# Attention block: first rows of maxima by TensorE transposes, a lead of 16 products, two half query groups moved into the loop, weight pieces held behind gathers

## The chip, the cores and the metric

The kernel runs on one core of a Trainium2 chip. The time is the device time of one execution in microseconds. The engines are TensorE (PE, matrix products), VectorE (DVE), ScalarE (ACT), GpSimd (POOL) and SyncE (SP, which issues transfers here). The profile is of one execution.

## The reference

One transformer block with conditioning: sequence 2048, width 512, 32 heads of 16 with one shared key and value head, and an inner width of 1376.

```
mod = (silu(c) @ w_mod).reshape(...)          # sa, ca, ga, sb, cb, gb
h = layernorm(x) * (1 + ca) + sa
q = (h @ wq) as 32 heads of 16;  k = h @ wk;  v = h @ wv
o = softmax(q k^T / sqrt(16)) v;  x = x + ga * (o @ wo)
h = layernorm(x) * (1 + cb) + sb
x = x + gb * (gelu(h @ w1 + b1) @ w2 + b2)
```

All is fp32. The kernel multiplies with numbers split in a high and a low part (names that end in H and L).

## The kernel before

**The units.** The attention is cut into 64 units: 8 blocks of 256 query rows, times 8 groups of 4 heads. A unit is worked in eight K steps. In a step PE computes four maximum products m (L507, queries times keys, only to find each row's maximum), which DVE reduces one by one (L512), and four score products e (L612), which ACT turns into exponentials (L616); sixteen accumulate instructions (L633) multiply these with the values. An e needs the row maxima inside its query operand: `qst` holds a unit's queries, and its partition rows 48 and 49 hold the negative maxima's high and low parts, so that the product subtracts them. The maximum products therefore run ahead of the scores by a lead, and the lead is made before the loop starts.

**From the maxima to the rows.** When all products of a unit are reduced, `put_max` orders: a DVE reduce to `mm` (L560), a 32x32 transpose to `turned` (L561), a gather on POOL to `mt` and its split to `mh` and `ml` (L555, L130, L137), and four transfers that SP issues into `qst` (L550). `later(n, f)` puts f off by n ticks of a clock that runs two to a K step. `MAX_WAIT` gives the waits ahead of gather and send.

**What sets the order.** Every engine works through its instructions in the order in which the program records them. SP's transfers stand in one row as well: one that waits holds all behind it. Beside the steps run other jobs as batches of matmuls in pieces: query projections (`qproj_late`), the output projection, transposes tp of the normalised rows xh, and the MLP's products w1ps and w2ps. A block's second layernorm, ahead of the MLP, runs on DVE (statistics, L840, L846) and POOL (ve, rs, xh, L847 to L852); tp reads xh, one half of the block's rows after the other.

**Weights in pieces.** The MLP's and output weights are loaded, scaled and split on POOL piece by piece inside the loop, one turn every `PREP` = 4 ticks. A turn loads one piece (for the last, narrower piece a POOL MEMSET ahead of the load, L1133, L1134) and splits an earlier one (L1137, L130, L137). The pieces share three buffers.

**The prologue.** Ahead of the loop, `SLOTS` deals the key and query projections, the small conditioning products (modl) and the first maximum products onto PE. `FIRST_MAX` orders the products of units 0 and 1, in pairs. `WARM[3]` filler matmuls (idle) stand ahead of the loop. The program before makes 56 maximum products there, the lead of `LEAD` = 6 groups of four behind unit 0's 32.

Of the kernel before, what the change touches and what calls it, by code (L numbers as in the profile page):

```python
# [14 lines left out]
P = 128  # L15
# [5 lines left out]

LEAD = 6
LEAD_0 = 6
FIRST_MAX = ((0, 0), (1, 0), (0, 1), (1, 1), (0, 2), (0, 3), (1, 2), (1, 3))
SLOTS = ((2, "keys 1", "keys 1"), (2, "keys 1", "keys 1"), (2, "low 1", "heads 2"), (2, "heads 2", "k 1"), (1, "warm"), (1, "heads 2"), (2, "heads 2", "v 0"),
# [4 lines left out]
MAX_WAIT = (1, 4)  # L30
QBUFS = 4
# [7 lines left out]
NORM_WAIT = 6  # L39
WARM = (4, 16, 2, 5)  # L40
MOD_WAIT = 3
# [9 lines left out]
def adaln_mqa_mlp(  # L51
# [88 lines left out]
    clock = [0]  # L140
    state = {"mods": False, "q": NB * KD, "busy": False, "turns": 1}
    pending = []
# [216 lines left out]

    def xhat1(b, eng):  # L360

        mv, rs, nm = hts_stats[b]
        xt = xts[b]
        for t in range(QT):
            if eng is nc.scalar:
# [50 lines left out]

    def send_q(b, g, qH, qL):
        for t, src in enumerate((qH, qL)):
            nc.sync.dma_start(out=dq[b][g][t].rearrange("a r j n -> (a r j) n"), in_=raw(src))
        state["q"] -= 1  # L420
        sent.add((b, g))

    sent = set()

    def qpairs(b, g):
        hH, hL = hts[b]
        gs = slice(g * P, (g + 1) * P)
        return [(wqH[:, k, gs], wqL[:, k, gs], hH[:, k, :], hL[:, k, :]) for k in range(KD)]

    def qtiles(b, g):  # L430
        qH = att.tile([P, BQ], F32R, name=f"qH{b}_{g}", tag="xH", bufs=2)
        qL = att.tile([P, BQ], F32R, name=f"qL{b}_{g}", tag="xL", bufs=2)
        return qH, qL
# [34 lines left out]
    def load_q(u):  # L468
# [5 lines left out]
        cols = slice(r0 % BQ, r0 % BQ + w)  # L474
        assert (h, g) in sent
        for s in range(2):
# [5 lines left out]
    class Max:  # L482


        def __init__(self):
# [45 lines left out]
    def put_max(u, mx):  # L531
# [13 lines left out]
        def send():  # L545
            for s in range(2):
                for r, src in ((48, mh), (49, ml)):
                    dst = qst[64 * s + r:64 * s + r + 1].rearrange("p j (t n) -> p (j t) n", n=P)
                    ring = nc.scalar if u == 0 and s else nc.sync
                    ring.dma_start(out=raw(dst), in_=raw(src[2 * T * s:2 * T * (s + 1), :].unsqueeze(1)))  # L550
            placed.add(u)
# [7 lines left out]
        def reduce():  # L559
            nc.vector.tensor_reduce(out=mm[:, :4 * T], in_=mx, axis=AX.X, op=ALU.max)  # L560
            nc.vector.transpose(out=turned, in_=mm)  # L561
# [669 lines left out]
    def q_group():  # L1231
        for i in range(KD):
            next(projections[0])
            if i == KD - 1:
                next(projections.pop(0))
            yield

    def warm():
# [24 lines left out]
    mod1(0, 3, act, dve)  # L1263
    rows = xhat1(1, act)
    run(rows, 2)

    def first_q(t):
        if t == 1:
            run(q_group())
            load_q(0)  # L1270
            load_q(1)

    stats1(2, first_q)
    run(rows)
    run(keys(0))
    low_k(0)
# [5 lines left out]
    def last_h(t):  # L1282
        if t == QT - 1:
# [9 lines left out]
            "v 0": one(v_out, 0), "v 1": one(v_out, 1), "v 2": one(v_out, 2), "v 3": one(v_out, 3), "rows": late_rows(),  # L1293
            "low 1": one(low_k, 1), "low 2": one(low_k, 2), "low 3": one(low_k, 3), "k 1": one(repeat_k, 1), "k 2": one(repeat_k, 2), "k 3": one(repeat_k, 3), "load": one(load_q, 2), "warm": warm(),
            "wq 1": one(prep_wq, 1), "wq 2": one(prep_wq, 2), "wq 3": one(prep_wq, 3)}
# [49 lines left out]
    def end_step(u, K):  # L1345

        pv(u, K)
        if K == steps[u] - 1:
            finish_unit(u)
            if units[u][1] == NQ - 1:  # L1350
                put_off(rest(units[u][0], units[u][0] == len(blocks) - 1))

    keep_warm(WARM[3], tag="e2", bufs=1)
    behind = None
    bare = [False]
    for u in range(NU):
        for K in range(0, steps[u], 2):
# [163 lines left out]
```

## Time and profile before

| | us |
|---|---|
| runs | 1563.49, 1561.64, 1562.66 (median 1562.66) |
| the profiled execution's own time | 1561.89 |
| its span in the trace | 1560.1 |
| PE busy | 1543.2 |
| DVE busy | 1400.8 |
| ACT busy | 1227.4 |
| POOL busy | 681.5 |

The times below are microseconds from the span's start. A row of a timeline gives the start, the time it took, the engine, the line of the code, the operation, output<-input, the shape of both, and how many alike instructions it joins; in square brackets how long the engine had been idle before, and what ended that. SPq is SP's queue, and its time is that of the issue with its waiting. A row of windows gives the stretch, its length, busy time and count of each engine, the granted TensorE clock, the share of the transfer engines and GB/s. With a line chosen, it counts that line alone.

### The profile page before, as it was taken

How to read it: one execution, taken by the hardware profiler on the slowest of the kernel's cores; microseconds unless marked ns; L12 is line 12 of the kernel's file. 1: busy time of each engine (PE TensorE's matmuls, PEld its weight loads, DVE VectorE, ACT ScalarE, POOL GpSimd, SP SyncE). 2: the span in 40 equal slices, each digit the busy share in tenths (PEclk: the TensorE clock that was granted, in tenths of full speed). 3: DMA queues.
4: the chain of work that ended last, by engine and by line, in shares of the span. 5: the costliest groups of instructions: out<-in, count | busy, mean ns of one | idle time of the engine just before them, and what ended most of it. 6: DMA issues, size and time to landing. Idle time of an engine off the chain costs nothing.

```text
span 1560.1 us, 41350 instructions
## 1 busy us (share of the span) xinstructions
PE 1543.2 (99%) x16347; PEld 955.2 (61%) x16347; DVE 1400.8 (90%) x2479; ACT 1227.4 (79%) x2392; POOL 681.5 (44%) x1194
## 2 busy tenths in 40 slices
PE   7999999999999999999999999999999999999999
PEld 4456555567655665557655675556655676556657
DVE  7999999999999999999999999999999999999725
ACT  5577778788878887788877887788877888778953
POOL 5545433867322570246522562245611474225721
PEclk9999999999999999999999999999999999999999
DMA  7225412312030211202012120302112120211241
GB/s 250 92 93 197 148 56 85 124 52 97 19 109 19 83 59 36 94 28 99 30 54 76 55 86 23 109 14 100 44 49 80 46 97 17 84 55 63 84 159 52
DMA packets 83125, 121.61 MB, mean 78 GB/s; under 512 B 19614, under 2 KB 56222, under 8 KB 82676
## 3 DMA queue, kind: packets, MB, share of 16 engines
q1 hardware_dynamic: 82916, 118.97, 22.9%
q8 instruction: 129, 2.11, 0.6%
q14 instruction: 64, 0.52, 0.1%
q10 hardware_dynamic: 16, 0.00, 0.0%
HBM read 91.13 MB, written 27.27 MB: 76 GB/s over the span
## 4 chain that ended last, share of the span: by engine, by line
PE 84%; DVE 10%; issue 3%; POOL 2%; DMA 1%; ACT 1%; SPq 0%; POOLq 0%; DVEq 0%
PE acc L633 28%; PE m L507 24%; PE e L612 15%; DVE mx L512 8%; PE w1ps L193 8%; PE w2ps L183 2%; PE w1ps L183 1%; DMA xt<-in_A_x_dram 1%; PE w2ps L193 1%; PE qps L193 1%; PE tp L193 1%; PE wops L193 1%; PE kps L162 1%; DVE st L840 1%; DVE x L833 1%
## 5 line engine op out<-in xcount | busy, mean ns | idle before, releaser
L512 DVE TENSOR_REDUCE mx<-m 128x1 f32<-128x512 f32 x2048 | 1269.3, 681 | 87.7 <-PE m L507 64.7
L616 ACT ACTIVATE p<-e 128x512 f32<-128x512 f32 x2048 | 1098.0, 598 | 254.8 <-PE e L612 106.4
L507 PE MATMUL m<-ks,qst 64*128 64x512 f32 x2048 | 832.9, 429 | 2.0 <-DVE mx L512 0.6
L612 PE MATMUL e<-qst,ks 64*128 64x512 f32 x2048 | 739.9, 413 | 0.0
L633 PE MATMUL acc<-p,va 128*32 128x256 f32 x8192 | 548.0, 385 | 0.0
L507 PEld LDWEIGHTS m<-ks,qst 64*128 64x128 f32 x2048 | 367.1, 184 | 211.6 <-DVE mx L512 174.0
L612 PEld LDWEIGHTS e<-qst,ks 64*128 64x128 f32 x2048 | 358.7, 185 | 92.3 <-ACT p L616 64.0
L633 PEld LDWEIGHTS acc<-p,va 128*32 128x32 f32 x8192 | 214.5, 109 | 213.7 <-issue 110.7
L555 POOL TENSOR_SCALAR mt<-turned 8x32 f32<-8x32 f32 x256 | 53.1, 208 | 419.5 <-DVE turned L561 407.4
L193 PE MATMUL w1ps<-h2H,w1t 64*128 64x256 f32 x1216 | 232.7, 287 | 0.0
L193 PEld LDWEIGHTS w1ps<-h2H,w1t 64*128 64x128 f32 x1216 | 183.6, 185 | 28.4 <-issue 14.4
L193 PE MATMUL w1ps<-h2L,w1t 64*128 64x256 f32 x608 | 167.0, 275 | 0.0
L193 PE MATMUL w2ps<-w2H,gH 64*128 64x512 f32 x264 | 115.9, 439 | 0.0
L193 PEld LDWEIGHTS w1ps<-h2L,w1t 64*128 64x128 f32 x608 | 112.8, 185 | 0.0
L193 PE MATMUL w2ps<-w2L,gH 64*128 64x512 f32 x264 | 103.4, 392 | 0.0
L193 PE MATMUL w2ps<-w2H,gL 64*128 64x512 f32 x264 | 103.0, 390 | 0.0
L959 POOL TENSOR_SCALAR tt<-tt 128x256 f32<-128x256 f32 x77 | 31.0, 403 | 143.1 <-ACT tt L958 109.8
L137 POOL TENSOR_TENSOR gL<-z,gH 128x256 fp32r<-128x256 f32 x77 | 56.9, 739 | 6.4
L960 POOL TENSOR_TENSOR tt<-tt,z 128x256 f32<-128x256 f32 x77 | 56.8, 738 | 6.4
L970 POOL TENSOR_TENSOR z<-tt,z 128x256 f32<-128x256 f32 x77 | 56.4, 733 | 6.0
L969 POOL TENSOR_TENSOR tt<-tt,z 128x256 f32<-128x256 f32 x77 | 56.5, 734 | 0.0
L193 PE MATMUL wops<-woH,onH 64*128 64x512 f32 x112 | 49.8, 444 | 0.0
(190 smaller groups left out, 1495.3 us busy)
## 6 DMA issues: line engine op xcount, KB each, us to landing
w1t<-dw SPq DMA_DIRECT2D x82, 512.0 KB
qst<-dq SPq DMA_DIRECT2D x384, 32.0 KB
do<-oc SPq DMA_DIRECT2D x64, 128.0 KB
dw<-w1s SPq DMA_DIRECT2D x11, 512.0 KB
xt<-in_A_x_dram SPq DMA_DIRECT2D x4, 1024.0 KB
dq<-qH SPq DMA_DIRECT2D x16, 256.0 KB
dq<-qL SPq DMA_DIRECT2D x16, 256.0 KB
x<-in_A_x_dram SPq DMA_DIRECT2D x8, 512.0 KB
```

The costliest lines, as they stand in the source:

```text
L137: eng_l.tensor_tensor(out=dst_l, in0=src, in1=raw(dst_h), op=ALU.subtract)
L183: nc.tensor.matmul(ps, a, b_, start=first_, stop=last_)
L193: ins = nc.tensor.matmul(ps, a[rows], b_[rows], start=first_ and s == 0, stop=last_ and s == 1)
L507: nc.tensor.matmul(m, qsts[u][rows, j, t * P:(t + 1) * P], ks[rows, kc * 512:(kc + 1) * 512], start=True, stop=True)
L512: nc.vector.tensor_reduce(out=self.mx[u][:, i, kc:kc + 1], in_=m, axis=AX.X, op=ALU.max)
L555: nc.gpsimd.tensor_scalar(out=mt[:, g:g + 32], in0=turned[g:g + 4 * T, :], scalar1=1.0, scalar2=0.0, op0=ALU.mult, op1=ALU.add)
L612: nc.tensor.matmul(e, ks[rows, kt * P:(kt + 1) * P], rhs, start=True, stop=True)
L616: ins = nc.scalar.activation(dst, e, AF.Exp, scale=0.25)
L633: ins = nc.tensor.matmul(accs[u][32 * cidx:32 * cidx + 32, :], va[:, kt, :], rhs, start=kt == 0, stop=kt == NKT - 1)
L960: nc.gpsimd.tensor_tensor(out=tt, in0=tt, in1=z, op=ALU.mult)
L969: nc.gpsimd.tensor_tensor(out=tt, in0=tt, in1=z, op=ALU.mult)
L970: nc.gpsimd.tensor_tensor(out=z, in0=tt, in1=z, op=ALU.add)
```

## The change

- `LEAD` goes from 6 to 4 groups: 48 products are made before the loop, not 56.
- `FIRST_MAX` gets counts, so that a part of a group can wait, and `SLOTS` a new order.
- Unit 0's rows no longer go over POOL and transfers: DVE writes mm and its rounding remainder into a cleared tile `spots`, four PE transposes (`rows0`) bring them to rows 48 and 49, and one DVE add puts these into `qst`.
- Query groups 0 and 1 of the first 512 rows are projected only for 256 columns before the loop; the other halves become two jobs of the loop.
- The gather is ordered directly behind the transpose, and the send two ticks later.
- A weight turn that comes due while a unit's maxima wait for their reduce (`closing`) is put off by one tick, behind the reduce and the gather.
- The filler matmuls ahead of the loop go; the first query and key projections alternate; the last slice of the second 512 rows' first layernorm goes to POOL.

```diff
-LEAD = 6
-LEAD_0 = 6
-FIRST_MAX = ((0, 0), (1, 0), (0, 1), (1, 1), (0, 2), (0, 3), (1, 2), (1, 3))
+LEAD = 4
+LEAD_0 = 4
+FIRST_MAX = ((0, 0, 4), (1, 0, 4), (0, 1, 4), (1, 1, 3), (0, 2, 4), (0, 3, 4), (1, 1, 1), (1, 2, 4), (1, 3, 4))
 SLOTS = ((2, "keys 1", "keys 1"), (2, "keys 1", "keys 1"), (2, "low 1", "heads 2"), (2, "heads 2", "k 1"), (1, "warm"), (1, "heads 2"), (2, "heads 2", "v 0"),
          (2, "heads 3"), (2, "heads 3"), (2, "heads 3"), (2, "heads 3"), (0, "keys 2"), (2, "keys 2"), (2, "keys 2"), (2, "keys 2"),
          (2, "low 2", "k 2", "v 1", "wq 1"), (0, "keys 3"), (2, "keys 3"), (2, "keys 3"), (2, "keys 3"), (2, "low 3", "k 3"),
-         (0, "v 2"), (2, "q 1"), (2, "q 1"), (2, "q 1"),
-         (2, "q 1", "rows"), (2, "v 3", "wq 2"), (2, "rows"), (2, "rows"), (2, "rows", "wq 3", "load"))
-MAX_WAIT = (1, 4)
+         (0, "v 2", "q 1", "q 1", "spots"), (2, "q 1", "q 1"), (2, "q 1"), (2, "rows", "wq 2"), (2, "wq 3"),
+         (2, "rows", "load"), (2, "v 3", "rows", "first", "rows"))
+MAX_WAIT = 2
...
-WARM = (4, 16, 2, 5)
+WARM = (4, 16, 2, 0)
...
     def qproj(b, g):
 
-        ps = psum.tile([P, BQ], F32, name=f"qps{b}_{g}", tag="v" if g else "x")
-        yield from mm3(ps, qpairs(b, g), 3, 1)
-        qH, qL = qtiles(b, g)
+        part = slice(0, HQ)
+        ps = psum.tile([P, HQ], F32, name=f"qps{b}_{g}", tag="v" if g else "x")
+        yield from mm3(ps, qpairs(b, g, part), 3, 1)
+        qH, qL = qtiles(b, g, part)
         if g == 0:
             nc.scalar.copy(qH, ps)
             nc.vector.tensor_tensor(out=qL, in0=ps, in1=raw(qH), op=ALU.subtract)
         else:
-            q32 = pro.tile([P, BQ], F32, name=f"q32_{b}_{g}", tag="h32", bufs=4)
+            q32 = pro.tile([P, HQ], F32, name=f"q32_{b}_{g}", tag="h32", bufs=4)
             nc.scalar.copy(q32, ps)
-            split(qH, qL, q32, act, pool)
-        send_q(b, g, qH, qL)
+            nc.scalar.copy(qH, q32)
+            yield -2
+            nc.gpsimd.tensor_tensor(out=qL, in0=q32, in1=raw(qH), op=ALU.subtract)
+        send_q(b, g, qH, qL, part)
         yield -2
 
-    def qproj_late(b, g):
-        ps = psum.tile([P, BQ], F32, name=f"qps{b}_{g}", tag="x")
-        size_ = BATCH if (b, g) < LONG else SHORT
-        yield from batches(ps, qpairs(b, g), size_)
-        q32 = wts_pool["rest"].tile([P, BQ], F32, name=f"q32_{b}_{g}", tag="ot", bufs=2)
+    def qproj_late(b, g, part=slice(0, BQ)):
+        w = part.stop - part.start
+        ps = psum.tile([P, w], F32, name=f"qps{b}_{g}_{part.start}", tag="x")
+        size_ = BATCH * BQ // w if (b, g) < LONG else SHORT
+        yield from batches(ps, qpairs(b, g, part), size_)
+        q32 = wts_pool["rest"].tile([P, w], F32, name=f"q32_{b}_{g}_{part.start}", tag="ot", bufs=2)
         if size_ == SHORT:
             nc.scalar.copy(q32, ps)
         else:
             nc.vector.tensor_copy(out=q32, in_=ps)
-        qH, qL = qtiles(b, g)
+        qH, qL = qtiles(b, g, part)
         split(qH, qL, q32, nc.gpsimd, nc.gpsimd)
-        later(4, lambda: send_q(b, g, qH, qL))
+        later(4, lambda: send_q(b, g, qH, qL, part))
...
-            begin = [o for u, kc in FIRST_MAX for o in products(u, [kc])]
+            parts = {(u, kc): products(u, [kc]) for u in range(2) for kc in range(NKC)}
+            begin = [parts[u, kc].pop(0) for u, kc, n in FIRST_MAX for _ in range(n)]
+            assert not any(parts.values())
...
+        if u == 0:
+            nc.vector.tensor_reduce(out=mm[:, :4 * T], in_=mx, axis=AX.X, op=ALU.max)
+            src = mm[:, :4 * T].rearrange("p (s n) -> p s n", s=2)
+            dst = spots.rearrange("p n (s c) -> p s n c", s=2)
+            nc.vector.tensor_copy(out=dst[:, :, :, 48], in_=src)
+            nc.vector.tensor_tensor(out=dst[:, :, :, 49], in0=src, in1=raw(dst[:, :, :, 48]), op=ALU.subtract)
+            return
         turned = att.tile([P, 32], F32, name=f"turned{u}", tag="turned", bufs=2)
-        if u == 0:
+        if u == 1:
...
-                    ring = nc.scalar if u == 0 and s else nc.sync
-                    ring.dma_start(out=raw(dst), in_=raw(src[2 * T * s:2 * T * (s + 1), :].unsqueeze(1)))
+                    nc.sync.dma_start(out=raw(dst), in_=raw(src[2 * T * s:2 * T * (s + 1), :].unsqueeze(1)))
...
             nc.vector.transpose(out=turned, in_=mm)
-            later(MAX_WAIT[0], gather)
-            later(MAX_WAIT[1], send)
+            gather()
+            state["closing"] = False
+            later(MAX_WAIT, send)
 
 
         if NQ <= u < NQ + 2:
             reduce()
         else:
+            state["closing"] = True
             later((0 - clock[0]) % 4 + 1, reduce)
+
+    spots = pro.tile([P, 4, P], F32R, name="spots")
+
+    def clear():
+        nc.gpsimd.memset(raw(spots), 0.0)
+
+    def first_rows():
+
+        qst = qsts[0].rearrange("p j n -> p (j n)")
+        ps = psum.tile([P, BQ], F32, name="rows0", **ebank())
+        for n in range(4):
+            nc.tensor.transpose(ps[:, n * P:(n + 1) * P], raw(spots[:, n, :]), ident)
+        nc.vector.tensor_tensor(out=qst, in0=ps, in1=raw(qst), op=ALU.add)
+        placed.add(0)
...
-    late = late[len(late) - len(projections):]
+    assert len(projections) == len(late) - 2
+    late = late[2:4] + [qproj_late(0, g, slice(HQ, BQ)) for g in range(2)] + late[4:]
...
+    def prepare_turn():
+        for _ in range(state["turns"]):
+            if weights and next(preps[weights[0]], 0) == 0:
+                weights.pop(0)
...
-                for _ in range(state["turns"]):
-                    if weights and next(preps[weights[0]], 0) == 0:
-                        weights.pop(0)
+                if state["closing"]:
+                    later(1, prepare_turn)
+                else:
+                    prepare_turn()
```

First place: DVE at the end of the prologue. mx0 are unit 0's maxima, m0 and m1 the products of units 0 and 1. Before:

```order
L512 TENSOR_REDUCE mx0_483<-m0_1_1_3_0_815 128x1
L512 TENSOR_REDUCE mx0_483<-m0_1_1_3_1_818 128x1
L560 TENSOR_REDUCE mm0_193<-mx0_483 128x8
L561 STREAM_TRANSPOSE turned0_821<-mm0_193 128x32
L512 TENSOR_REDUCE mx1_545<-m1_0_0_2_0_843 128x1
L512 TENSOR_REDUCE mx1_545<-m1_0_0_2_1_846 128x1
```

After:

```order
L520 TENSOR_REDUCE mx0_484<-m0_1_1_3_0_809 128x1
L520 TENSOR_REDUCE mx0_484<-m0_1_1_3_1_812 128x1
L547 TENSOR_REDUCE mm0_193<-mx0_484 128x8
L550 CAST spots_197<-mm0_193 128x2x4
L551 TENSOR_TENSOR spots_197<-mm0_193,spots_197 128x2x4
L520 TENSOR_REDUCE mx1_546<-m1_1_1_1_0_828 128x1
L520 TENSOR_REDUCE mx1_546<-m1_1_1_1_1_831 128x1
L598 TENSOR_TENSOR qst0_158<-rows0_844,qst0_158 128x512
L520 TENSOR_REDUCE mx1_546<-m1_0_0_2_1_868 128x1
```

The transpose to turned0 is gone, three operations into mm0 and spots take its place, and the add of rows0 stands two reduces later.

Second place: POOL around block 0's second layernorm (ve0_0 to xh2_0_0). mt11 to ml11 are unit 11's gather, w2f8 and w2f6 weight pieces. Before:

```order
L555 TENSOR_SCALAR mt11_4472<-turned11_4471 8x32 x4
L130 TENSOR_SCALAR mh11_4473<-mt11_4472 8x128
L137 TENSOR_TENSOR ml11_4474<-mt11_4472,mh11_4473 8x128
L1137 TENSOR_TENSOR w2f8_4398<-w2f8_4398,gb_83 128x512
L130 TENSOR_SCALAR w2H_3816<-w2f8_4398 128x512
L137 TENSOR_TENSOR w2L_3817<-w2f8_4398,w2H_3816 128x512
L1133 MEMSET w2f10_4580 128x512
L847 TENSOR_SCALAR ve0_0_4222<-mv0_0_4220 128x2
L849 TENSOR_TENSOR rs0_0_4221<-ve0_0_4222,mhalf_64 128x2
L852 TENSOR_SCALAR xh2_0_0_4218<-x1_0_4210,mv0_0_4220,rs0_0_4221 128x512 x2
```

After:

```order
L569 TENSOR_SCALAR mt11_4577<-turned11_4576 8x32 x4
L130 TENSOR_SCALAR mh11_4578<-mt11_4577 8x128
L137 TENSOR_TENSOR ml11_4579<-mt11_4577,mh11_4578 8x128
L1167 TENSOR_TENSOR w2f6_4419<-w2f6_4419,gb_83 128x512
L130 TENSOR_SCALAR w2H_3986<-w2f6_4419 128x512
L137 TENSOR_TENSOR w2L_3987<-w2f6_4419,w2H_3986 128x512
L877 TENSOR_SCALAR ve0_0_4229<-mv0_0_4227 128x2
L879 TENSOR_TENSOR rs0_0_4228<-ve0_0_4229,mhalf_64 128x2
L882 TENSOR_SCALAR xh2_0_0_4225<-x1_0_4217,mv0_0_4227,rs0_0_4228 128x512 x2
```

The gather and one weight piece still stand in a row ahead of ve0_0, but two K steps of products lie between unit 11's maxima before and now; the piece is w2f6, since later ones were put off, and the MEMSET of w2f10 is gone from here.

Third place: that MEMSET, on POOL around unit 12's gather, and on SP the transfers that follow it. POOL after:

```order
L569 TENSOR_SCALAR mt12_4916<-turned12_4915 8x32 x4
L130 TENSOR_SCALAR mh12_4917<-mt12_4916 8x128
L137 TENSOR_TENSOR ml12_4918<-mt12_4916,mh12_4917 8x128
L1167 TENSOR_TENSOR w2f7_4505<-w2f7_4505,gb_83 128x512
L130 TENSOR_SCALAR w2H_3986<-w2f7_4505 128x512
L137 TENSOR_TENSOR w2L_3987<-w2f7_4505,w2H_3986 128x512
L1167 TENSOR_TENSOR w2f8_4626<-w2f8_4626,gb_83 128x512
L130 TENSOR_SCALAR w2H_3986<-w2f8_4626 128x512
L137 TENSOR_TENSOR w2L_3987<-w2f8_4626,w2H_3986 128x512
L1163 MEMSET w2f10_4977 128x512
```

SP before:

```order
L651 DMA do1_115<-oc0_1266 128x256
L550 DMA qst0_158<-mh12_4811 1x4x128
L550 DMA qst0_158<-ml12_4812 1x4x128
L550 DMA qst0_158<-mh12_4811 1x4x128
L550 DMA qst0_158<-ml12_4812 1x4x128
```

SP after:

```order
L681 DMA do1_115<-oc0_1231 128x256
L1164 DMA w2f9_4972<-in_B_w2_dram 128x512
L1164 DMA w2f10_4977<-in_B_w2_dram 96x512
L564 DMA qst0_158<-mh12_4917 1x4x128
L564 DMA qst0_158<-ml12_4918 1x4x128
```

In SP's row the loads of w2f9 and w2f10 moved from ahead of unit 11's sends (mh11) to ahead of unit 12's (mh12). The load of w2f10 writes the tile that the MEMSET clears, which POOL reaches behind unit 12's gather and the pieces w2f7 and w2f8.

More of the change, by code (lines that the diff above doesn't have):

```diff
@@ L140, in adaln_mqa_mlp @@
     clock = [0]
-    state = {"mods": False, "q": NB * KD, "busy": False, "turns": 1}
+    state = {"mods": False, "q": NB * KD + 2, "busy": False, "turns": 1, "closing": False}
     pending = []
@@ L358, in stats1, with xhat1 @@
         hts_stats[b] = mv, rs, nm
-    def xhat1(b, eng):
+    def xhat1(b, eng, last=None):
         mv, rs, nm = hts_stats[b]
@@ L364, in xhat1 @@
         for t in range(QT):
+            eng = last if last and t == QT - 1 else eng
             if eng is nc.scalar:
@@ L415, in v_out, with send_q, qpairs, qtiles @@
         nc.scalar.copy(va[:, b * QT:(b + 1) * QT, 0:Dh], pv_[:, :, 16:32])
-    def send_q(b, g, qH, qL):
+    def send_q(b, g, qH, qL, part):
         for t, src in enumerate((qH, qL)):
-            nc.sync.dma_start(out=dq[b][g][t].rearrange("a r j n -> (a r j) n"), in_=raw(src))
+            nc.sync.dma_start(out=dq[b][g][t][:, :, :, part].rearrange("a r j n -> (a r j) n"), in_=raw(src))
         state["q"] -= 1
-        sent.add((b, g))
+        sent.update((b, g, n) for n in range(part.start, part.stop, HQ))
     sent = set()
-    def qpairs(b, g):
+    def qpairs(b, g, part):
         hH, hL = hts[b]
         gs = slice(g * P, (g + 1) * P)
[L428 to L433, printed above, removed]
+        return [(wqH[:, k, gs], wqL[:, k, gs], hH[:, k, part], hL[:, k, part]) for k in range(KD)]
+    def qtiles(b, g, part):
+        w = part.stop - part.start
+        qH = att.tile([P, BQ], F32R, name=f"qH{b}_{g}_{part.start}", tag="xH", bufs=2)
+        qL = att.tile([P, BQ], F32R, name=f"qL{b}_{g}_{part.start}", tag="xL", bufs=2)
+        return qH[:, :w], qL[:, :w]
     def qproj(b, g):
-        ps = psum.tile([P, BQ], F32, name=f"qps{b}_{g}", tag="v" if g else "x")
-        yield from mm3(ps, qpairs(b, g), 3, 1)
-        qH, qL = qtiles(b, g)
+        part = slice(0, HQ)
+        ps = psum.tile([P, HQ], F32, name=f"qps{b}_{g}", tag="v" if g else "x")
+        yield from mm3(ps, qpairs(b, g, part), 3, 1)
+        qH, qL = qtiles(b, g, part)
         if g == 0:
@@ L443, in qproj @@
         else:
-            q32 = pro.tile([P, BQ], F32, name=f"q32_{b}_{g}", tag="h32", bufs=4)
+            q32 = pro.tile([P, HQ], F32, name=f"q32_{b}_{g}", tag="h32", bufs=4)
             nc.scalar.copy(q32, ps)
-            split(qH, qL, q32, act, pool)
-        send_q(b, g, qH, qL)
+            nc.scalar.copy(qH, q32)
+            yield -2
+            nc.gpsimd.tensor_tensor(out=qL, in0=q32, in1=raw(qH), op=ALU.subtract)
+        send_q(b, g, qH, qL, part)
         yield -2
-    def qproj_late(b, g):
-        ps = psum.tile([P, BQ], F32, name=f"qps{b}_{g}", tag="x")
-        size_ = BATCH if (b, g) < LONG else SHORT
-        yield from batches(ps, qpairs(b, g), size_)
-        q32 = wts_pool["rest"].tile([P, BQ], F32, name=f"q32_{b}_{g}", tag="ot", bufs=2)
+    def qproj_late(b, g, part=slice(0, BQ)):
+        w = part.stop - part.start
+        ps = psum.tile([P, w], F32, name=f"qps{b}_{g}_{part.start}", tag="x")
+        size_ = BATCH * BQ // w if (b, g) < LONG else SHORT
+        yield from batches(ps, qpairs(b, g, part), size_)
+        q32 = wts_pool["rest"].tile([P, w], F32, name=f"q32_{b}_{g}_{part.start}", tag="ot", bufs=2)
         if size_ == SHORT:
@@ L474, in load_q @@
         cols = slice(r0 % BQ, r0 % BQ + w)
-        assert (h, g) in sent
+        assert (h, g, cols.start) in sent
         for s in range(2):
@@ L1234, in q_group @@
             if i == KD - 1:
-                next(projections.pop(0))
+                last = projections.pop(0)
+                next(last)
             yield
+        next(last, None)
+        yield
     def warm():
@@ L1263, in adaln_mqa_mlp @@
     mod1(0, 3, act, dve)
-    rows = xhat1(1, act)
-    run(rows, 2)
+    first_group, first_keys = q_group(), keys(0)
+    for _ in range(KD - 1):
+        next(first_group)
+        next(first_keys)
     def first_q(t):
         if t == 1:
-            run(q_group())
+            run(first_group)
             load_q(0)
             load_q(1)
+            run(xhat1(1, act, pool))
+            run(first_keys)
     stats1(2, first_q)
-    run(rows)
-    run(keys(0))
     low_k(0)
@@ L1293, in adaln_mqa_mlp @@
             "v 0": one(v_out, 0), "v 1": one(v_out, 1), "v 2": one(v_out, 2), "v 3": one(v_out, 3), "rows": late_rows(),
-            "low 1": one(low_k, 1), "low 2": one(low_k, 2), "low 3": one(low_k, 3), "k 1": one(repeat_k, 1), "k 2": one(repeat_k, 2), "k 3": one(repeat_k, 3), "load": one(load_q, 2), "warm": warm(),
+            "low 1": one(low_k, 1), "low 2": one(low_k, 2), "low 3": one(low_k, 3), "k 1": one(repeat_k, 1), "k 2": one(repeat_k, 2), "k 3": one(repeat_k, 3), "load": one(load_q, 2), "warm": warm(), "first": one(first_rows), "spots": one(clear),
             "wq 1": one(prep_wq, 1), "wq 2": one(prep_wq, 2), "wq 3": one(prep_wq, 3)}
```

## The prediction

> **What bounds the kernel now.** I read the page's busy times and chain first.
>
> ```profile
> span 1560.1 us, 41350 instructions
> PE 1543.2 (99%) x16347; PEld 955.2 (61%) x16347; DVE 1400.8 (90%) x2479; ACT 1227.4 (79%) x2392; POOL 681.5 (44%) x1194
> PE 84%; DVE 10%; issue 3%; POOL 2%; DMA 1%; ACT 1%; SPq 0%; POOLq 0%; DVEq 0%
> ```
>
> PE is busy 99% of the span, so the loop ends when PE's instructions have been issued one after another; POOL is idle more than half the time but can still be late at one place. The next view, windows that count the accumulate instructions (16 to a K step), gives a step's price.
>
> ```profile
> 253.44:284.79 31.35, 12.84 (x192) 5.02 (x193) 1.00 0.35 111
> 339.89:396.90 57.01, 21.42 (x321) 8.38 (x321) 1.00 0.26 90
> 1471.10:1476.29 5.19, 2.14 (x33) 0.84 (x33) 1.00 0.02 4
> ```
>
> 192 accumulates are 12 plain steps: 31.35 / 12 = 2.61 us. 320 are 20 steps with twelve 256-column matmuls beside them: 57.01 / 20 = 2.85. Two late steps that have no maximum products left but the same twelve cost 5.19. The third figure from the right is the granted clock, 1.00.
>
> The third view is the engines' timelines where the prologue ends, with the tensor-engine row that I use for a transpose.
>
> ```profile
> 27.54 0.66 PE L375 MATMUL tp<-ident,xt 128*128 128x128 f32 x4 [1.25 <-ACT h L381]
> ...
> 60.62 5.22 DVE L512 TENSOR_REDUCE mx<-m 128x1 f32<-128x512 f32 x8
> 66.89 2.48 DVE L512 TENSOR_REDUCE mx<-m 128x1 f32<-128x512 f32 x4 [1.05 <-PE m L507]
> 69.40 0.19 DVE L560 TENSOR_REDUCE mm<-mx 128x8 f32<-128x32 f32 x1
> 69.93 1.01 POOL L555 TENSOR_SCALAR mt<-turned 8x32 f32<-8x32 f32 x4 [0.32 <-DVE turned L561]
> 72.14 0.61 SPq L550 DMA_DIRECT2D qst<-ml  x1
> 73.59 1.43 PE L287 MATMUL idle<-wkH 128*128 128x512 f32 x5
> 74.95 0.49 PE L612 MATMUL e<-qst,ks 64*128 64x512 f32 x2
> ```
>
> Reduces run at 5.22 / 8 = 0.65 us nearly back to back: before the loop VectorE paces, not PE. Unit 0's rows take from 69.40 to the end of the sends (72.75 here), and the first score e stands at 74.95, behind five filler matmuls.
>
> **The prologue.** All of unit 0's maxima are reduced at the 46th product instead of the 48th, and the split query groups and the later place of the small matmuls take the 1.05 us hole out of VectorE's row: the reduce mm moves from 69.40 to about 69.40 − 2 × 0.65 − 1.05 = 67.0. Then three small DVE operations (0.2 each, by the mm row), four PE transposes (0.66, the row at 27.54) behind the two products and one group that stand ahead of them (about 1), and one DVE add of 128x512, whose nearest row, the 0.65 reduce over the same elements, prices it at 0.7: 67.0 + 0.6 + 0.7 + 1.0 + 0.7 = 70.0. The first e moves from 74.95 to about 70.0: **−5.0 us**. It can't come to more than the work removed ahead of the loop plus that hole: eight reduces fewer (56 to 48 products, 8 × 0.65 = 5.2) and 1.05, so 6.3; if the transposes wait one more group of 1 us or so on either side, 3.5. The five fillers go too: they only filled the wait for the rows. What is late next at that place is the DVE add itself, the last thing the first e needs.
>
> **The loop's step mix.** In PE's program order plain steps go from 40 to 36; four steps carry the two query halves left over, as twelve 256-column matmuls; two late bare steps with such a batch become full ones. 4 × (2.85 − 2.61) + (2 × 2.85 − 5.19) = 0.96 + 0.51: **+1.5 us**. The eight reduces that went into the loop lie inside these step prices. The new halves' copies, splits and four stores lie beside PE on DVE, POOL and SP; were that cover gone, four stores at 0.61 would add 2.4.
>
> **Block 0's normalised rows wait on POOL.** Lead shorter by eight products means two steps less between a unit's maxima and its first e. Unit 11's gather, and a weight piece that is now held behind it, stand on POOL ahead of the second layernorm as today, but come two steps later.
>
> ```profile
> 306.12 0.21 DVE L561 STREAM_TRANSPOSE turned<-mm 128x32 f32<-128x32 f32 x1
> 311.99 0.41 DVE L840 BATCH_NORM_STATS2 st<-x 128x6 f32<-128x256 f32 x1
> ...
> 306.42 1.01 POOL L555 TENSOR_SCALAR mt<-turned 8x32 f32<-8x32 f32 x4 [0.96 <-DVE turned L561]
> 308.31 1.26 POOL L1137 TENSOR_TENSOR w2f<-w2f,gb 128x512 f32<-128x512 f32 x1
> 311.58 0.53 POOL L1133 MEMSET w2f<- 128x512 f32 x1
> 312.73 0.24 POOL L847 TENSOR_SCALAR ve<-mv 128x2 f32<-128x2 f32 x1 [0.61 <-DVE mv L846]
> 313.89 4.14 POOL L852 TENSOR_SCALAR xh<-x,mv,rs 128x512 f32<-128x512 f32 x2
> ...
> 319.43 0.49 PE L193 MATMUL tp<-ident,xh 64*128 64x128 f32 x3
> 319.98 0.38 PE L193 MATMUL tp<-ident,xh 64*128 64x128 f32 x2
> ```
>
> A gather takes 308.31 − 306.42 = 1.9, a weight piece 311.58 − 308.31 = 3.3. DVE reduces unit 11's maxima right after the last BATCH_NORM_STATS2 (312.4), turned ends at 312.4 + 0.5 = 312.9. POOL: gather to 314.8, piece w2f6 to 318.1, ve and rs (1.16, from 312.73 to 313.89) to 319.3, first half of xh to 321.4, second to 323.4. PE wants the first at 319.43 and the second at 319.98. The second is late by **+3.4 us**, once. Its lower bound is 0.1, if the piece were not in front of ve (323.4 − 3.3 against 319.98); no row makes it dearer than one more 0.3 for a small DVE operation ahead of turned, 3.7.
>
> **The same in blocks 1 to 6, without a piece.**
>
> ```profile
> 491.96 0.42 DVE L840 BATCH_NORM_STATS2 st<-x 128x6 f32<-128x256 f32 x1
> 493.86 4.15 POOL L852 TENSOR_SCALAR xh<-x,mv,rs 128x512 f32<-128x512 f32 x2
> 499.96 0.38 PE L193 MATMUL tp<-ident,xh 64*128 64x128 f32 x2
> ```
>
> There turned ends at 492.4 + 0.5 = 492.9, the gather at 494.8, ve and rs at 496.0, xh at 500.1, while PE wants the second half at 499.8 (the group at 499.96 is already in it). 0.3 x 6 blocks = **+1.8 us**; between 0 and 3.
>
> **Unit 12's rows wait on SP behind a weight load.**
>
> ```profile
> 301.21 11.27 SPq L1134 DMA_DIRECT2D w2f<-in_B_w_dram  x2
> 312.56 0.66 SPq L550 DMA_DIRECT2D qst<-mh  x1
> 315.18 2.38 SPq L478 DMA_DIRECT2D qst<-dq  x3
> ...
> 327.77 0.21 DVE L561 STREAM_TRANSPOSE turned<-mm 128x32 f32<-128x32 f32 x1
> 333.14 0.74 POOL L137 TENSOR_TENSOR h2L<-h,h2H 128x256 fp32r<-128x256 f32 x1
> 341.23 0.39 PE L612 MATMUL e<-qst,ks 64*128 64x512 f32 x1
> ```
>
> Today the load of the last w2 piece blocks SP until POOL's MEMSET has ended (311.58 + 0.53 = 312.1), and the row sends start at 312.56, last to 315.18. In the new order that load stands ahead of unit 12's sends, and its MEMSET behind unit 12's gather and two held pieces. Unit 12's turned, two steps later (2.7 each, between the plain and the laden price above), ends at 327.98 + 5.4 = 333.4; POOL has finished h2 by then (333.88 with the gather still inside it, so 1.9 earlier without). Gather to 335.4, pieces w2f7 and w2f8 (2 × 3.3) to 342.0, MEMSET to 342.5, first send 0.45 later, four sends 2.62, landing. The landing isn't shown alone: it is more than nothing, and at most 74.95 − 72.75 = 2.2 in the prologue, where fillers cover it; I take 0.9. The rows are there at 342.5 + 0.45 + 2.6 + 0.9 = 346.5, against an e at 341.23: **+5.3 us**, once (4.4 to 6.6). PE takes its instructions in order, so maxima, accumulates and everything else wait too.
>
> **The clock after that hole.**
>
> ```profile
> 8.26 5.22 PE L292 MATMUL modr<-wm,csb 128*32 128x512 f32 x16 [8.26 <-DMA wm<-in_w_mod_dram]
> 8.20:11.55 3.35, 3.29 (x8) 0.77 (x10) 1.00 1.07 375
> 11.55:13.40 1.85, 1.85 (x10) 0.37 (x6) 1.00 1.16 289
> ```
>
> The sixteen first matmuls come after 8.26 us of idle PE. Eight begin in the first 3.35 us, the other eight in the next 1.85 (two of the ten counted there began before); the slow start costs 1.5 us, though the printed clock stays 1.00. After the 1.25 us hole at 27.54 four transposes take 0.66, as fast as elsewhere. A hole of 5.3 lies between, nearer the long one: **+1.0** of 0 to 1.5. The holes of 2.0 and 1.4 in which the 3.4 above falls lie near the short one: 0. The Trainium skill, "TensorE: Matmul & The Clock Gate", Part 1, says that the array falls to half clock after an idle window of about 3.4 us, on a window that runs freely, and needs about as long to recover. The trace's first matmuls agree. By that rule the hole costs either nothing or 1.6 to 1.7, as an estimate from the page, and the sum would be 1.0 lower or 0.7 higher.
>
> **Sum.** −5.0 + 1.5 + 3.4 + 1.8 + 5.3 + 1.0 = +8.0 on the profiled execution's own 1561.89, so 1569.9; the runs' median, 1562.66, lies 0.8 above it. I take 1570.2. A measurement here can tell about 0.2%, 3.1 us.
>
> **Rivals.**
> *POOL is in time (faster).* Place: POOL's queue around units 11 and 12. If the held weight pieces (3.3 and 6.6 us there) don't reach the path, the 3.4, 1.8, 5.3 and 1.0 go and 1562.66 − 5.0 + 1.5 = 1559.2 is left, 1558 with a prologue gain of 6. It decides from the point where POOL's MEMSET ends by 341.23 − 0.45 − 2.6 − 0.9 = 337.3, five us earlier than I make it. For it: POOL's 44%. Against it: its order is fixed, and each duration used is a row. 0.18.
> *Only one of the two holes.* The wait for xh would hold POOL's next work but not the load, or the load would be issued earlier: 8.0 − 3.4 or 8.0 − 6.3, so 1564.4 to 1567.3. 0.2.
> *The shorter lead is late again and again.*
>
> ```profile
> 440.54 0.21 DVE L561 STREAM_TRANSPOSE turned<-mm 128x32 f32<-128x32 f32 x1
> 447.76 0.65 SPq L550 DMA_DIRECT2D qst<-mh  x1
> ```
>
> Unit 12 has 341.23 − 327.98 = 13.3 us from turned to its e, after the change 13.3 − 5.3 = 8. Unit 17 today takes 447.76 + 2.6 + 0.9 − 440.75 = 10.5, since SP has the block's row sums in front. If those loads moved along with turned, seven such units would lose 2.5 each: +17, 1587. I think they stand at their old times, so that they are past when turned comes two steps later. 0.07.
> The forecast itself gets 0.55.
>
> **Range and chances.** Below, POOL in time reaches down to 1558; above, the forecast with its dear ends (prologue 1.5 less, unit 12 +1.3, blocks +1.2, clock +0.5) is 1574.7. 1558 to 1575 leaves out the repeated lateness and the low tail. Faster by over 0.2% (under 1559.5): a good half of POOL in time, 0.10, and 0.04 from the forecast's cheap ends with a larger prologue gain, 0.14. Within: the rest of POOL in time, half of one hole and 0.02 of the forecast, 0.20. Slower: the other half of one hole (0.10), the repeated lateness (0.07) and the rest of the forecast (0.49), 0.66.
>
> **What the changed profile would show.** First e near 70 and a DVE add there; PE with a hole of about 2 and one of 1.4 at transposes of xh, on POOL's xh, near 315; PE with one hole of some 5 us at unit 12's e, near 340, SP's wait on POOL for w2f longer than 11 us; plain steps 2.61 elsewhere. PE holes of 0.3 at six later xh. The forecast is wrong if POOL's MEMSET ends before unit 12's turned has aged 4 us, if many units show holes at their first e, or if the first e stands after 72.

## The result

The changed kernel is slower. The median of six runs is 1573.42 us (1571.6 to 1577.59), against 1561.65 us (six runs, 1561.53 to 1563.49) for the kernel before; the ratio is 1.0074, with a 95% interval of 1.0061 to 1.0087. The forecast was 1570.2. The profiled execution took 1572.07, its span is 1570.3, and 10.2 us more than before are to be found in it.

The page of the changed kernel: the span, the busy times, the chain of work that ended last, and the group of the score products with the idle time ahead of it.

```profile
span 1570.3 us, 41473 instructions
PE 1544.5 (98%) x16406; PEld 957.9 (61%) x16406; DVE 1401.8 (89%) x2483; ACT 1228.5 (78%) x2391; POOL 685.5 (44%) x1194
PE 86%; DVE 5%; issue 4%; POOL 3%; DMA 1%; ACT 1%; SPq 0%; POOLq 0%; DVEq 0%; ACTq 0%
L642 PE MATMUL e<-qst,ks 64*128 64x512 f32 x2048 | 743.1, 412 | 5.6 <-DMA qst<-ml 5.6
```

PE's busy time hardly changed (1543.2 before), so the loss is idle time, and the idle time of a whole group of 2048 score products is one wait of 5.6. PE's waits say where:

```profile
PE e L642 <- DMA qst<-ml: 5.6, 1, 5.6
PE tp L193 <- POOL xh L882: 2.7, 2, 1.4
```

One wait of a score for its rows of maxima, and two of transposes for xh; the kernel before has neither.

**The prologue** (timelines where it ends):

```profile
67.08 0.19 DVE L547 TENSOR_REDUCE mm<-mx 128x8 f32<-128x32 f32 x1
68.52 0.66 PE L597 MATMUL rows<-ident,spots 128*128 128x128 f32 x4
69.21 0.69 DVE L598 TENSOR_TENSOR qst<-rows,qst 128x512 fp32r<-128x512 f32 x1 [0.26 <-PE rows L597]
70.10 0.50 PE L642 MATMUL e<-qst,ks 64*128 64x512 f32 x2
```

The first score stands at 70.10 where it stood at 74.95: 4.85 gained.

**Block 0's second layernorm** (POOL and PE):

```profile
308.78 1.02 POOL L569 TENSOR_SCALAR mt<-turned 8x32 f32<-8x32 f32 x4 [8.22 <-DVE turned L575]
315.28 4.15 POOL L882 TENSOR_SCALAR xh<-x,mv,rs 128x512 f32<-128x512 f32 x2
...
317.42 0.37 PE L193 MATMUL tp<-ident,xh 64*128 64x128 f32 x1 [1.40 <-POOL xh L882]
319.49 0.37 PE L193 MATMUL tp<-ident,xh 64*128 64x128 f32 x1 [1.33 <-POOL xh L882]
```

Gather, weight piece, then xh: its halves are ready at 317.4 and 319.4, and PE stands until each. The first row holds a second reading: POOL had idled 8.2 us just before, so it was not short of time but had its work in an unlucky order.

**Unit 12** (DVE, POOL, SP and PE):

```profile
332.70 0.21 DVE L575 STREAM_TRANSPOSE turned<-mm 128x32 f32<-128x32 f32 x1
341.67 0.57 POOL L1163 MEMSET w2f<- 128x512 f32 x1
342.27 0.33 SPq L1164 DMA_DIRECT2D w2f<-in_B_w_dram  x1
342.69 0.65 SPq L564 DMA_DIRECT2D qst<-mh  x1
346.45 0.76 PE L642 MATMUL e<-qst,ks 64*128 64x512 f32 x1 [5.57 <-DMA qst<-ml]
```

The maxima are turned at 332.9, and POOL has made mh of them by 334.6. But SP has stood at the two weight loads since 322.3; the last of these waits for the MEMSET, and only behind it do the rows go, from 342.69. The steps around it, from windows that count the accumulates (the granted clock is the third figure from the right):

```profile
314.29:320.36 6.07, 1.07 (x16) 0.42 (x17) 1.00 0.13 32
339.38:349.53 10.15, 1.07 (x17) 0.42 (x17) 0.78 0.13 34
349.53:353.42 3.89, 1.93 (x16) 0.59 (x16) 0.71 0.60 182
500.47:503.47 3.00, 1.07 (x16) 0.41 (x16) 1.00 0.02 6
```

The step of the xh waits takes 6.07, 3.3 more than its 2.77 before; unit 12's first 10.15 instead of 2.85; the next 3.89, in which sixteen accumulates take 1.93 instead of 1.07 at a printed clock of 0.71; and a step of block 1 (the last row) 3.00 instead of 2.67.

### The profile page after: what moved, and what is told of

It is laid out like the page before. It is cut to its first block, busy times and chain, and to the rows that moved or that the text cites. A ratio compares the mean times of both kernels' runs of the same rounds, so it can differ in the third digit from the quotient of the medians.

```text
span 1570.3 us, 41473 instructions
## 1 busy us (share of the span) xinstructions
PE 1544.5 (98%) x16406; PEld 957.9 (61%) x16406; DVE 1401.8 (89%) x2483; ACT 1228.5 (78%) x2391; POOL 685.5 (44%) x1194
## 4 chain that ended last, share of the span: by engine, by line
PE 86%; DVE 5%; issue 4%; POOL 3%; DMA 1%; ACT 1%; SPq 0%; POOLq 0%; DVEq 0%; ACTq 0%
PE acc L663 29%; PE m L515 24%; PE e L642 16%; PE w1ps L193 8%; DVE mx L520 4%; PE w2ps L183 2%; PE w2ps L193 2%; PE qps L193 1%; PE wops L193 1%; PE w1ps L183 1%; PE tp L193 1%; PE kps L162 1%; POOL w2L L137 1%; POOL w2f L1167 1%; PE tp L376 0%
## 5 line engine op out<-in xcount | busy, mean ns | idle before, releaser
L193 PE MATMUL w1ps<-h2H,w1t 64*128 64x256 f32 x1232 | 236.7, 288 | 0.0
L193 PEld LDWEIGHTS w1ps<-h2H,w1t 64*128 64x128 f32 x1232 | 186.8, 185 | 28.8 <-DVE mx L520 19.8
```

Of the source, the lines that this page charges most:

```text
L193: ins = nc.tensor.matmul(ps, a[rows], b_[rows], start=first_ and s == 0, stop=last_ and s == 1)
```

## The experiments

Where nothing else is said, the edit is to the changed kernel.

**Weight turns never put off.**

```diff
-                if state["closing"]:
+                if False:
```

> The changed kernel, with weight turns never put off. My theory (order and rows decide): w2f6 then comes ahead of unit 11's gather, so the second layernorm's xh is on time and the 3.3 us hole at tp goes; at unit 12, POOL now has w2f7, w2f8 and the MEMSET ahead of mt12 instead of behind ml12, so the rows still come some 5 us late by the gather, and the hole with its slow clock stays: about 3 to 4 us faster than the changed kernel, 1568 to 1570. Rival theory (holding the pieces is the cause of both holes): both go, 11 to 12 us faster, about 1561.

Measured: 1569.08 us, ratio to the kernel before 1.0045 (1.0032 to 1.0057). PE's waits:

```profile
PE e L642 <- DMA qst<-ml: 5.8, 2, 4.7
```

No xh wait is left, and unit 12's is, 4.7 long; the pieces now stand ahead of its gather. (The other wait for rows, 1.1, is at unit 10, whose gather also fell behind a piece.) So the hole at xh needs the held turns. It needs the later gather too: with the lead of 24 (below) the turns are held and xh is in time.

**Turns put off by four ticks.**

```diff
-                    later(1, prepare_turn)
+                    later(4, prepare_turn)
```

> The changed kernel, with a due weight turn put off by four ticks instead of one, so that on SP the four row sends of a unit stand ahead of the piece's load, and w2f6 stands behind xh on POOL. My theory: both holes go (3.3 at xh, 5.6 at unit 12 and about 2.8 of slow clock behind it): 11 to 12 us faster than the changed kernel, 1560.5 to 1562, about the kernel before. Rival: the pieces w2f7 to w2f10 only move later and hold POOL's gelu work back by several us instead, so 3 to 6 us of the gain are lost again: 1564 to 1568.

Measured: 1568.87 us, ratio 1.0041 (1.0027 to 1.0055). My theory fell, and the rival was right, with more than it put on it. The rows were sent in time, and the hole came back one step later under another name (POOL, ACT and PE):

```profile
345.92 0.72 POOL L990 TENSOR_TENSOR tt<-tt,z 128x256 f32<-128x256 f32 x1
346.68 0.42 ACT L993 ACTIVATE tt<-tt 128x256 f32<-128x256 f32 x1 [6.28 <-POOL tt L990]
347.63 0.79 PE L642 MATMUL e<-qst,ks 64*128 64x512 f32 x1 [6.09 <-ACT p L646]
```

POOL works through w2f7 to w2f10 and reaches the first gelu's tt only at 345.9; ACT waits in its order with the exponentials behind, and PE for a free score bank. What is late is the whole train of w2 pieces.

**The lead of 24 back.**

```diff
-LEAD = 4
-LEAD_0 = 4
+LEAD = 6
+LEAD_0 = 6
```

> The changed kernel with the lead of 24 products back, all else kept. My theory: the gathers of units 11 and 12 come two steps earlier, SP sends unit 12's rows ahead of the last loads, both holes go (11.6), the 0.33 us in seven steps where DVE has statistics and mm together go (2.3), the prologue gives back its eight reduces (5): 8 to 9 us faster than the changed kernel, 1563 to 1565. Rival (the late weights of the q halves are enough for the hole, whatever the lead): the hole at unit 12 stays, and the kernel is 0 to 3 us slower or faster than the changed one.

Measured: 1573.49 us, ratio 1.0069 (1.0056 to 1.0082): nothing gained. No score waits for its rows, and xh is on time, but the same gelu hole stands at 350.5:

```profile
349.59 0.42 ACT L993 ACTIVATE tt<-tt 128x256 f32<-128x256 f32 x1 [4.57 <-POOL tt L990]
350.54 0.79 PE L642 MATMUL e<-qst,ks 64*128 64x512 f32 x1 [4.35 <-ACT p L646]
```

The lead was not enough of an explanation. The prologue gave back 3.3 (first e at 73.40), and the first steps behind it 0.9 more, at a granted clock of 0.50 from 73.7 to 77.1. The 0.33 us in the statistics steps went from block 0 and blocks 2 to 6. From here my theory was another: the two query halves finish two loop rounds later, the w2 pieces start only when the last query projection is through, so they run two turns late into whatever is next: unit 12's rows, or the gelu.

**The query groups whole, no halves in the loop.**

```diff
-    state = {"mods": False, "q": NB * KD + 2,
+    state = {"mods": False, "q": NB * KD,
...
-        part = slice(0, HQ)
-        ps = psum.tile([P, HQ], F32, name=f"qps{b}_{g}", tag="v" if g else "x")
+        part = slice(0, BQ)
+        ps = psum.tile([P, BQ], F32, name=f"qps{b}_{g}", tag="v" if g else "x")
...
-    late = late[2:4] + [qproj_late(0, g, slice(HQ, BQ)) for g in range(2)] + late[4:]
+    late = late[2:]
```

> The changed kernel with query groups 0 and 1 projected whole before the loop, and no halves in it. My theory: the w2 pieces come two turns earlier, so that unit 12's sends have no weight load ahead of them and the 8.3 us there go; at block 0's second layernorm the held piece is w2f8 with the MEMSET, xh comes 3.9 late, and unit 11's sends wait behind the last load inside the same hole; the loop saves 1.0, the prologue costs up to 1.5 more: 7 to 9 us faster than the changed kernel, 1564 to 1566. Rival (the halves don't matter for the weights): hole at unit 12 stays, within 1 us of the changed kernel.

Measured: 1568.97 us, ratio 1.0044 (1.0032 to 1.0057). Nothing waits near unit 12 any more. The pieces are two turns earlier, and the held one with the MEMSET now delays unit 11's rows and xh together:

```profile
PE e L642 <- DMA qst<-ml: 2.4, 2, 1.7
PE tp L193 <- POOL xh L882: 0.3, 1, 0.3
```

That step takes 7.01 and the next 3.76, some 5.3 more than in the kernel before, where I had expected 3.9: the granted clock is 0.50 from 321.6 to 325.0, behind three waits of 1.7, 0.7 and 0.3. That is 1.4 of the 3 us by which the run missed my range. The first e is at 71.68: whole groups cost 1.6 in the prologue.

**Only the late start, in the kernel before.**

```diff
-            if state["mods"] and state["q"] == 0 and w2H is None:
+            if state["q"] == 0:
+                state["ready"] = state.get("ready", 0) + 1
+            if state["mods"] and state.get("ready", 0) > 2 and w2H is None:
```

> The kernel before, and nothing else changed but that the w2 pieces start two turns later. My theory: the last load stands ahead of unit 12's sends here too, its MEMSET behind w2f7 and w2f8: rows at about 345 against an e at 341.2, a hole of about 4, then the gelu behind w2f9 and w2f10 for 2 to 3 more, and a slow clock of 1 to 3: 7 to 10 us slower than before, 1569 to 1572. Rival (it takes the shorter lead and the held turns as well): within 1 us of the kernel before.

Measured: 1568.75 us, ratio 1.0042 (1.003 to 1.0055), 0.3 less than the range expected. One edit that touches neither lead nor rows gives more than half of the loss:

```profile
PE e L612 <- DMA qst<-ml: 3.8, 1, 3.8
```

The rows of unit 12 wait as computed; no wait for the gelu shows. That step takes 8.42 and the next 4.18, for 2.85 each, so 3.1 more than the wait; the granted clock is 0.50 until 351.8.

**Only the lead, in the kernel before** (`LEAD` and `LEAD_0` from 6 to 4 there).

> The kernel before with the lead of 16 products and nothing else. My theory: the first e can move only as far as the rows by POOL and transfers allow, from 74.95 to about 74.2, so that the shorter lead gains under 1 us in the prologue; steps with statistics and mm together cost 7 x 0.35; unit 12's gather now falls behind w2f9 and w2f10 on POOL, its rows come at about 346 against an e at 341: a hole of 5 and slow steps of 1 to 3 behind it. In all 7 to 10 us slower than before: 1569 to 1572. Rival (the shorter lead is harmless where no piece is held and no half group is late): 1560 to 1563.

Measured: 1574.6 us, ratio 1.008 (1.0067 to 1.0094), slower than expected.

```profile
PE e L612 <- DMA qst<-ml: 5.7, 3, 4.2
```

Its timeline:

```profile
74.81 0.57 PE L612 MATMUL e<-qst,ks 64*128 64x512 f32 x2 [0.96 <-DMA qst<-ml]
347.72 0.47 PE L612 MATMUL e<-qst,ks 64*128 64x512 f32 x1 [4.18 <-DMA qst<-ml]
```

The first e waits for its rows at 74.81, so that the shorter lead by itself gains 0.1 in the prologue, or 0.7 counted from this run's own mm at 69.93. (Half a microsecond is no difference here: in the six traces with the changed prologue the first e stands between 69.52 and 70.10.) What I had not expected is the clock: it is 0.50 from 78.6 to 82.0, and the step there takes 4.40 instead of 2.98. Unit 12 waits 4.2, here because its gather stands behind w2f9 and w2f10. So in the kernel before a hole at unit 12 has two causes, each enough alone: pieces two turns late, or a lead two steps shorter with the pieces where they were. In the changed kernel, with its held turns, neither was enough: with the lead of 24 (late pieces alone) and with whole groups (short lead alone) unit 12's rows come in time.

**Unit 0's rows by transfers, all else as changed.**

```diff
-        if u == 0:
-            nc.vector.tensor_reduce(out=mm[:, :4 * T], in_=mx, axis=AX.X, op=ALU.max)
...
-            return
...
-        if NQ <= u < NQ + 2:
+        if u == 0:
+            nc.vector.tensor_reduce(out=mm[:, :4 * T], in_=mx, axis=AX.X, op=ALU.max)
+            nc.vector.transpose(out=turned, in_=mm)
+            gather()
+            send()
+        elif NQ <= u < NQ + 2:
             reduce()
...
```

> The changed kernel with unit 0's rows by gather on POOL and four transfers as before (two on ACT's queue), and no TensorE transposes; the lead of 16 stays. My theory: mm at 67.1, gather to 69.5, sends to 71, rows at about 72: the first e 1.5 to 2.5 later than 70.1, the run about 2 us slower than the changed kernel, so that the transposes are worth 2 of the 4.8 us of the prologue and the shorter lead the rest. Rival (the shorter lead alone brings the prologue's gain): the first e within 0.5 of 70.1.

Measured: 1577.77 us, ratio 1.0098 (1.0083 to 1.0114).

```profile
72.66 0.86 PE L636 MATMUL e<-qst,ks 64*128 64x512 f32 x2 [3.40 <-DMA qst<-ml]
```

The first e is 2.56 later than with transposes, about as expected. The run lost 4.3 where I had put 2: the granted clock is 0.50 from 71.5 to 78.3, which adds 1.2 up to the end of the first full step (3.38 instead of 2.98), and the step behind the xh waits ran at a slow clock too (below). Of the 4.85 of the prologue, 2.6 hang on the transposes.

**PE kept at work through the hole of the changed kernel.**

```diff
+            if u == 12 and "filled" not in state:
+                state["filled"] = True
+                fill = psum.tile([P, 512], F32, name="fill12", tag=f"e{bank}", bufs=1)
+                for _ in range(24):
+                    nc.tensor.matmul(fill, ks[0:64, 0:P], ks[0:64, 0:512], start=True, stop=True)
             e = psum.tile([P, 512], F32, name=f"e{u}_{K}_{j}_{s}", tag=f"e{bank}", bufs=1)
```

> The changed kernel with 24 matmuls on the keys, into the next score bank and read by nobody, ahead of unit 12's first e, so that PE works through the hole. My theory (PE runs at half clock for some 5 us after the hole): the hole stays 5.6 to 6 long, the steps behind it take 2.85 again, 2.5 to 3 us faster than the changed kernel, 1570.5 to 1571. Rival (the slow steps come from DVE or ACT catching up): no gain.

Measured: 1570.85 us, ratio 1.0053 (1.0041 to 1.0066), 2.6 below the changed kernel's median.

```profile
341.46 5.65 PE L640 MATMUL fill<-ks 64*128 64x512 f32 x24
347.31 0.46 PE L647 MATMUL e<-qst,ks 64*128 64x512 f32 x1 [0.20 <-DMA qst<-ml]
```

Its windows:

```profile
346.00:349.00 3.00, 2.80 (x23) 2.06 (x22) 0.96 (x2) 1.09 (x2) 2.83 (x4) 1.00 0.11 32
...
320.00:322.00 2.00, 2.00 (x18) 0.82 (x12) 0.72 (x2) 0.72 (x2) 1.28 (x2) 0.50 0.00 0
```

The first e comes 7.07 after the start of its step, as in the changed kernel, and the clock behind it is 1.00. The two steps take 12.1 together instead of 14.0, so the clock was worth 1.9 of the 2.8. The other 0.9 stays at full clock, against my theory: the second step takes 3.33, not 2.85, and in it a score waits 0.23 for ACT, whose exponentials stand behind a gelu activation that waits for POOL's tt. That the medians differ by just the 2.6 that I had expected is in part chance: the profiled spans differ by 1.6, as 1.5 was lost again at the place of the last line, to which I come back.

**Two turns doubled, in the idle time of POOL.** With the put-off of four ticks, and:

```diff
-        for _ in range(state["turns"]):
+        state["w2 turns"] = state.get("w2 turns", 0) + (weights[0] == "w2")
+        for _ in range(2 if state["w2 turns"] in (4, 5) and weights[0] == "w2" else state["turns"]):
```

> The put-off of four ticks, and besides two of the w2 turns (the fourth and fifth) do two pieces instead of one, into the 8 us in which POOL idles ahead of unit 11's gather, so that the pieces are where they were in the kernel before. My theory now (the two half query groups start the w2 pieces two turns later, and these then run into whatever comes next: unit 12's rows or the first gelu): no hole at xh, at unit 12 or at the gelu, 11.6 us faster than the changed kernel: 1561 to 1562.5, within 0.1% of the kernel before. Rival (the shorter lead itself leaves the rows late): a hole of 3 us or more at unit 11 or 12 stays, 1565 or more.

Measured: 1561.51 us, ratio 0.9994 (0.9985 to 1.0002): all of the loss is gone, and the time is that of the kernel before. One hole of over half a microsecond is left in the loop, at unit 13's first maximum product:

```profile
319.13 0.52 POOL L1163 MEMSET w2f<- 128x512 f32 x1
319.68 0.35 SPq L1164 DMA_DIRECT2D w2f<-in_B_w_dram  x1
327.06 0.47 PE L515 MATMUL m<-ks,qst 64*128 64x512 f32 x1 [1.05 <-DMA qst<-dz]
```

**And each turn's load ordered ahead of its split.**

```diff
-            if 1 <= i < n + 1:
-                work(i - 1)
             for k in range(ahead) if i == 0 else (i + ahead - 1,):
                 if k < n:
                     load(k)
+            if 1 <= i < n + 1:
+                work(i - 1)
             yield
```

> The version with the doubled turns, and each weight turn now orders its load (with the MEMSET of the last piece) ahead of its split. In the version before it PE waited 1.05 us for unit 13's queries, whose load on SP stood behind the last weight load, and that behind the MEMSET at 319.1. Here the MEMSET stands one piece (3.3) earlier, at 315.8: that hole goes, 1 us faster, 1560 to 1561, 0.1% faster than the kernel before. Rival (another load or engine holds unit 13's queries): the hole stays, no change.

Measured: 1560.48 us, ratio 0.999 (0.9981 to 0.9999). The hole is gone, and this version is the fastest of all, 1.4 us or 0.1% below the kernel before; the interval just clears 1.

## Why the prediction was right, and where it was not

**Direction and place.** The time lies in the range, and the two one-off holes stand where the forecast put them, for the reasons that it gave: xh behind a gather and a held piece, and unit 12's rows behind a load behind a MEMSET. The size was short: +8.0 was forecast for the profiled execution, and 10.2 came.

**Term by term**, in the profiled execution:

| term | forecast | measured | read from |
|---|---|---|---|
| prologue | −5.0 | −4.85 | first e 74.95 to 70.10 |
| step mix | +1.5 | +1.5 | four steps with halves 11.40 in all, two late steps 2.85 each |
| xh, block 0 | +3.4 | +3.3 | 6.07 − 2.77 |
| blocks 1 to 6 | +1.8 | +2.0 | six times 3.00 − 2.67 |
| unit 12's hole | +5.3 | +5.6 | the wait of 5.57 |
| clock behind it | +1.0 | +2.8 | 10.15 − 2.85 − 5.57 + 3.89 − 2.84 |

They sum to +10.3, against 10.2 between the spans; what is left (+0.3 in block 0's statistics step, +0.2 at the last unit, and small gains in other steps) about cancels.

**The clock was mis-sized.** The step that failed is the price of the slow steps after the hole, 1.0 of 0 to 1.5, taken from the kernel's first matmuls. Measured: 2.8, of which the run with fillers puts 1.9 on the clock, so either way outside my bounds. In the first matmuls eight ran slowly for 3.35 us; here PE works at 0.50 from 346.45 to about 351.8, 5.3 us. One window of it:

```profile
348.00:350.00 2.00, 2.00 (x19) 1.33 (x20) 1.39 (x3) 0.96 (x2) 1.92 (x3) 0.50 0.18 46
```

The other 0.9 had no term: in the run with fillers it stays at a clock of 1.00, in part as a wait for ACT behind the gelu; what the rest is stays open. The 1.6 to 1.7 that stands beside the term in the prediction is nearer, and too small for the whole as well. For the two holes at xh I had put the clock at 0, and in the changed kernel's trace it is; that was luck, since in two other runs the same two waits were followed by 0.50 (last section).

**Right size, wrong cause: blocks 1 to 6.** I had xh late there by 0.3. PE's waits name xh only twice, both in block 0. The 0.33 stands two steps earlier, where DVE now does its statistics and the unit's mm and turned in one stretch:

```profile
499.66 0.41 DVE L870 BATCH_NORM_STATS2 st<-x 128x6 f32<-128x256 f32 x1
499.99 0.17 DVE L574 TENSOR_REDUCE mm<-mx 128x8 f32<-128x32 f32 x1
500.26 0.21 DVE L575 STREAM_TRANSPOSE turned<-mm 128x32 f32<-128x32 f32 x1
500.40 0.24 DVE L876 BATCH_NORM_AGGREGATE mv<-st 128x2 f32<-128x12 f32 x2
500.56 4.82 DVE L520 TENSOR_REDUCE mx<-m 128x1 f32<-128x512 f32 x8
```

DVE has no gap in these rows; four reduces of 0.6 fill a plain step of 2.61 but for 0.2, so that the 0.38 of mm and turned, which fell two steps earlier before, is added to a full step. With the lead of 24 the steps of blocks 0 and 2 to 6 cost what they did before, which fits; that DVE is the cause is read from its rows, and no run took an operation out of them.

**What the forecast didn't see: what stood behind the holes.** Its list of next bottlenecks ended with unit 12. Two runs that removed the wait for unit 12's rows (four ticks, the lead of 24) found the gelu's one step later, about as costly. My explanation of the place was right, but the common root, the start of the w2 pieces after the last query projection, lay in a rule of the planner that I had read only as an order of rows. The rival that POOL would be in time is refuted at both places; but its ground, that POOL has time to spare, is what the two doubled turns used.

**The repeated lateness** did not come: no score but unit 12's waits for its rows in the changed kernel. The remaining 1.35 between the profiled execution and the median of the runs isn't in that trace; the last section has a likely cause.

## What to carry to other kernels

When a change moves one job, look at what starts when it ends: here two small projections, cheap where they stood, delayed the weight pieces behind them by two turns, and that cost more than the prologue gained. SP's queue, which works in order, passed one load's wait on to four small sends behind it, some 8 us here, so ask of each hole what the next in the row was waiting for; curing the visible wait alone moved the hole by one step, at about the same price. Idle time on an engine can pay for it: two turns doubled where POOL idled, together with the put-off of four ticks, brought the time from 1573.42 back to 1561.51.

## What the runs showed of the chip that I had not expected

A hole can cost more than its length: after 5.6 us without a matmul PE ran at a granted 0.50 for 5.3 us, and the two steps cost 2.8 beyond the wait, some 1.9 of it by the clock. The price isn't fixed: in the run with rows by transfers a wait of 5.5 at the same place was followed by only 3.2 us of work at 0.50 and cost 1.8 beyond it. Between the first matmuls and the tail, each stretch at 0.50 in these traces lasts 3.4 or 6.8 us.

And the hole needn't be one piece. In the changed kernel's trace the two waits at xh, 1.40 and 1.33 with 0.7 of work between, left the clock at 1.00. In the run with fillers the same two waits were followed by a granted 0.50 (the window 320.00 to 322.00 shown there), and the step behind took 4.17 instead of 2.71; the run with rows by transfers shows the same. The Trainium skill, "TensorE: Matmul & The Clock Gate", Part 1, has a window of about 3.4 us that runs freely and says that idle windows close the gate: a free phase fits that the same waits sometimes cost 1.4 more, though here PE was not idle for a whole window. It would also fit the spread of the changed kernel's runs, 1571.6 to 1577.59, where those of the kernel before beside them lie within 2 us; the slowest has a mean granted clock of 0.994, the profiled one 0.998. Which steps of it ran slowly isn't on record.
